# Second half of a fused kernel on one core: instruction order from a list of deadlines, four more buffers, and weight sums one stage behind

## The chip, the cores and the metric

One core of a Trainium2 chip runs the whole program; the other cores are idle. The metric is the device time of one execution in microseconds (us), and the kernel before stands at 1070.38 us (median of 3 runs, 1067.11 to 1073.82). All times below that are not called medians come from one profiled execution of the kernel before.

## What is computed

Three stages follow each other on 2304 tokens of width 512.

```
# attention: 4 batches, 8 heads, 576 positions, head size 64
out_up    = repeat(softmax(q4 @ k4.T / 8) @ v4, 4)   # q4, k4, v4: means of 4 neighbours
out_local = softmax(q @ k.T / 8 where |i-j| < 4) @ v
x = out_up + out_local                               # [2304, 512]
# gated FFN, 512 -> 1536 -> 512
xn = x / sqrt(mean(x*x) + 1e-6) * rms_g
x  = (silu(xn @ w_gate) * (xn @ w_val)) @ w_out
# squared-relu FFN, 512 -> 2048 -> 512
r  = maximum(x @ w_in, 0)
y  = (s * r * r + b) @ w_out2
```

Weights arrive in double precision. The kernel widens them on the chip and splits every number into two halves of 16 bits, a high and a low one, so a product costs three matmuls (high·high, high·low, low·high).

## The kernel before

**Tiling.** Tokens are worked in 8 blocks of 288 (TB), each as two halves of 144 (HB). The middle of x is kept transposed in Xf (4 row tiles of 128, trace name X).

**First part.** Attention for 4 batches runs as generators beside the first gated FFN. The FFN's blocks 0 and 1 run together, 2 to 5 one after the other (`middle`), 6 and 7 together (`mains`). A gate or value tile is 12 matmuls at L577, the elementwise work on it is at L584, L585 and L187 (ScalarE ACT, VectorE DVE), the output tiles are 36 matmuls each at L599, and a row sum `sn` per block (L619, reduced at L621) gives the block's scale `xsc`. From step START_W of the middle blocks on (`open_w2`), TensorE (PE), ACT and DVE run in the order in which the code issues them; before that a scheduler orders ACT and DVE.

**Side work.** Beside blocks 2 to 7, `side_work` prepares the second FFN's weights in 8 parts q (0 to 3 are w_in, 4 to 7 are w_out2). A part is: four raw pieces (a DMA at L476 into one of three staging buffers, two ACT instructions L480 and L481, two DVE instructions L485 and L487; piece n+3 is fetched only when piece n is through DVE), block sums t1, t3, t2 (DVE L887, L888, L895) for a product scheme with 7 instead of 8 block products, 16 small matmuls into `st` (L894) whose row maximum `mi` (L898) gives a power-of-two scale (L181 to L183), a last block sum (L899), and 14 conversions into halves, each one ACT instruction (L133) and one DVE instruction (L134) that depend on each other. All steps of a part are issued before the next part's raw pieces, except that the next part's first ACT pair is issued after conversion 10. `side_step` issues a side step at 2 of 3 FFN steps and later at each. `open_at` holds the parts 4 to 7 back until the first FFN has done with the storage they overwrite.

**Second part.** Per block, the in stage computes 4 groups p (512 columns of the hidden layer each) with 7 products of 12 matmuls each (`product`, L1012, 128x128 weights on 144 columns). The products accumulate in three PSUM banks per group (pa and pb from a pool of 4, pc from a pool of 2). ACT copies pa (L1042 or L1026), DVE adds to the banks' contents (L1017, reads pb and pc), ACT applies relu and square (L1026, L1027; in odd groups one square is on DVE), and the combinations (L1017, L1020, L1024) are turned into halves `G` ("put": ACT L133, DVE L134). The y stage has 7 products of 4x12 matmuls on G, in banks ya, yd, yb, yc; results leave through ACT (L1096) and a DMA (L1098). `x_parts` builds the next block's operand xo from Xf during the y stage. Only PE is in hand order here; the scheduler orders ACT and DVE. Groups 2 and 3 use three scratch buffers of groups 0 and 1 again (SETS: SL[1], SL[3], SL[4] and SL[6], SL[8], SL[9]), so their first writes wait for the last put of group 0 or 1. A bank of pb or pc is used by PE again only when DVE has read its earlier content. The side work's last steps are issued between the products of block 0.

Of the kernel before, what the change touches and what calls it, by code (L numbers as in the profile page):

```python
# [8 lines left out]
F32 = mybir.dt.float32  # L9
# [15 lines left out]
TB = 288  # L25
# [23 lines left out]
START3 = 16  # L49
START_W = 84  # L50
# [29 lines left out]
def kernel(  # L80
# [751 lines left out]
    def side_work():  # L832
# [26 lines left out]
        for n in range(3):  # L859
            issue(n)  # L860
        yield
        for q in range(8):
            c = chain(q)
            for kc in range(KC):
                n = q * KC + kc
                while not open_at(q, "raw", kc):
                    yield
                if n not in acted:
                    first(n)
                    yield  # L870
                if kc < 3:
                    first(n + 1)
                if wide:
                    widen_dve(stgs[n % 3], c.f32(kc * 512, 512))
                issue(n + 3)
                if q >= 4:
                    f = c.f32(kc * 512, 512)
                    if n == 16:
                        pool.tensor_copy(out=tail["csum"], in_=f)
                    else:  # L880
                        pool.tensor_tensor(out=tail["csum"], in0=tail["csum"], in1=f, op=ALU.add)
                yield
            while not open_at(q, "T"):
                yield
            r = c.f32(0, PART).rearrange("p (u c) -> p u c", c=256)
            t1, t2, t3, b22 = r[:, 8:10], r[:, 10:12], r[:, 12:14], r[:, 5:8:2]
            dve.tensor_tensor(out=t1, in0=r[:, 1:4:2], in1=r[:, 0:3:2], op=ALU.subtract)  # L887
            dve.tensor_tensor(out=t3, in0=r[:, 1:4:2], in1=b22, op=ALU.subtract)  # L888
            yield
# [5 lines left out]
            dve.tensor_tensor(out=t2, in0=b22, in1=t1, op=ALU.subtract)  # L895
            yield
            mi = p1.tile([128, 1], F32, tag="mi", name="mi")
            dve.tensor_reduce(out=mi, in_=st, axis=AX.X, op=ALU.max)  # L898
            dve.tensor_tensor(out=r[:, 1:4:2], in0=r[:, 4:7:2], in1=t2, op=ALU.subtract)  # L899
# [66 lines left out]
    if True:  # L966
# [17 lines left out]
        for _ in xparts:  # L984
            pass

    order[0].__exit__(None, None, None)
    tail["m2"].__exit__(None, None, None)
    order[0] = tc.manual_schedule(engines={pe.engine})
    order[0].__enter__()  # L990
# [4 lines left out]
    SL = [s12[:, i] for i in range(12)] + [R[:, 6112:6400], tail["csum"][:, :TB]]  # L995
# [6 lines left out]
    def product(ps, i, w, x, first, last_):  # L1002

        b = UNIT[PAIRS[i][1]]
        n = len(x)
        for j in range(n):
            for m in range(2):
                for k in range(2):
                    for lw, lx in ((0, 0), (0, 1), (1, 0)):
                        t, o = w[j]  # L1010
                        a = 2 * o + b[k] * 512 + lw * 256 + 128 * m
                        pe.matmul(out=ps[:, m, :], lhsT=t[:, a:a + 128], rhs=x[j][:, i, lx, k, :],  # L1012
                                  start=first and j == m == k == lw == lx == 0,
                                  stop=last_ and j == n - 1 and k == 1 and lw == 1, skip_group_check=True)
# [4 lines left out]
    def sub(o, a, b):
        dve.tensor_tensor(out=o, in0=a, in1=b, op=ALU.subtract)  # L1020

    def square(o, src, eng):
        if eng is dve:
            dve.scalar_tensor_tensor(out=o, in0=src, scalar=0.0, in1=src, op0=ALU.max, op1=ALU.mult)  # L1024
        else:
            act.activation(out=o, in_=src, func=AF.Relu)  # L1026
            act.activation(out=o, in_=o, func=AF.Square)  # L1027

    def in_stage(blk):

        def put(p, i, src):
            halves(G[p][:, i, 0], G[p][:, i, 1], src, gsc[:, p:p + 1], dve)

        def group(p):
            s = [two(t) for t in SETS[p]]
            w, x = [(W2h, p * PART)], [xo]
            a, b = (mmp.tile([128, 2, HB], F32, tag="mm", name="p" + n) for n in "ab")
            c = pC.tile([128, 2, HB], F32, tag="c", name="pc")
            product(a, 0, w, x, True, False)
            product(b, 1, w, x, True, False)  # L1040
            product(c, 2, w, x, True, False)
            act.activation(out=s[0], in_=a, func=AF.Copy)  # L1042
            add(s[2], b, s[0])
            yield
            product(b, 3, w, x, False, False)
            product(a, 4, w, x, False, True)
            add(s[3], b, s[0])
            add(s[3], c, s[3])
            square(s[1], a, act)
            put(p, 0, s[1])  # L1050
            yield
            product(c, 5, w, x, False, True)
            product(b, 6, w, x, False, True)
            square(s[3], s[3], act)
            put(p, 6, s[3])
            add(s[0], b, s[0])
            add(s[2], c, s[2])
            square(s[2], s[2], dve if p % 2 else act)
            put(p, 4, s[2])
            square(s[0], s[0], act)  # L1060
            yield
            sub(s[1], s[0], s[1])
            add(s[4], s[0], s[3])
            add(s[3], s[3], s[1])
            put(p, 1, s[3])
            put(p, 2, s[4])
            sub(s[2], s[2], s[3])
            put(p, 5, s[2])
            put(p, 3, s[1])

        rest_ = []
        for p in (0, 2):
            pair = [group(p), group(p + 1)]
            for k in range(3):
                for g in pair:
                    next(g)
                    yield
                if k == 0:
                    for g in rest_:
                        next(g, None)  # L1080
            rest_ = pair
        later.extend(rest_)

    later = []

    def y_stage(blk):
        t0 = blk * TB
        w = [(W1h, PART * p) for p in range(3)] + [(Rh, 0)]
        keep = p1.tile([128, 2, TB], F32, tag="x2", name="keep")
        s1, c21 = two(keep[:, 0]), two(keep[:, 1])  # L1090
        v, c22 = two(SETS[0][0]), two(SETS[0][2])

        def emit(c, r, src):
            ys = two(p1.tile([128, TB], F32, tag="u", name="ys", bufs=3))
            for m in range(2):
                act.activation(out=ys[:, m], in_=src[:, m], func=AF.Identity,  # L1096
# [109 lines left out]
```

## Time and profile before

| | |
|---|---|
| median of 3 runs | 1070.38 us (1067.11 to 1073.82) |
| profiled execution | 1075.27 us, span of its trace 1073.5 us |
| PE busy | 961.5 us, 90% of the span |
| PE weight loads (beside the matmuls) | 826.6 us, 77% |
| DVE busy | 714.1 us, 67% |
| ACT busy | 605.3 us, 56% |
| POOL busy | 270.8 us, 25% |
| DMA | 61.44 MB, 18% of the queues' span |

Busy times are sums over the span, and overlapped pieces of pipelined matmuls count once. What counts for a change is not an engine's share of the whole span but, in each stretch, who waits for whom. In the rows further on, a bracket like [4.39 <-DVE R L1017] says that the engine stood idle for 4.39 us before that instruction, and that a DVE instruction of line 1017 with output R ended the wait. PEclk is the clock granted to PE, 1.00 being 2.4 GHz. W, W1 and R are the large SBUF tensors that hold weights, halves and scratch buffers.

### The profile page before, as it was taken

Reading aid. Unit: us, or ns where it says so; the run is one execution under the profiler, and the core shown is the slowest. Engines: PE = TensorE matmul, PEld = TensorE weight load, DVE = VectorE, ACT = ScalarE, POOL = GpSimd, SP = SyncE. Lnnn points to the kernel's source line nnn. Section 1 sums busy time; section 2 is a strip of 40 time slices with the busy share of each in tenths; the row PEclk is TensorE's granted clock in tenths of the full one; section 3 lists DMA queues with packets and bytes.
Section 4 is the critical chain, followed back from the end, with each engine's and each line's share of the span. In section 5 each row is a group of like instructions: output and inputs, shape, how many; then the busy total and the mean of one; then the engine's idle time right before and its main releaser. Section 6 shows DMA issues by size and latency. Waiting matters only on the chain.

```text
span 1073.5 us, 27144 instructions
## 1 busy us (share of the span) xinstructions
PE 961.5 (90%) x11342; PEld 826.6 (77%) x11347; DVE 714.1 (67%) x1652; ACT 605.3 (56%) x1486; POOL 270.8 (25%) x356
## 2 busy tenths in 40 slices
PE   5965999989999999999899887798989898989987
PEld 3654776768877888877678765798989898988887
DVE  4997986754443441577767787967585958586674
ACT  2865685634434442456544556757574847566573
POOL 7524754544463333311114331000000000000000
PEclk8976999999999999999989998989989998999899
DMA  8873054211111000131212230000000000000000
GB/s 241 274 220 121 20 158 141 81 46 47 46 40 54 13 2 1 60 99 40 80 40 79 60 87 33 2 8 18 19 7 24 2 24 2 24 7 18 7 19 24
DMA packets 25579, 61.44 MB, mean 57 GB/s; under 512 B 3216, under 2 KB 11408, under 8 KB 25456
## 3 DMA queue, kind: packets, MB, share of 16 engines
q1 hardware_dynamic: 25456, 59.70, 18.3%
q8 instruction: 89, 1.46, 0.6%
q14 instruction: 34, 0.28, 0.1%
HBM read 54.97 MB, written 4.72 MB: 56 GB/s over the span
## 4 chain that ended last, share of the span: by engine, by line
PE 58%; DVE 22%; ACT 9%; DMA 6%; issue 3%; POOL 2%; SPq 0%; ACTq 0%; DVEq 0%; POOLq 0%
PE mmb L577 14%; DVE W L134 8%; PE mmb L599 7%; PE yc L1012 5%; PE ya L1012 4%; PE yb L1012 4%; PE pb L1012 4%; PE pc L1012 4%; DVE R L1017 3%; ACT W L133 3%; PE m2b L577 3%; PE yd L1012 2%; PE pa L1012 2%; DMA R<-in_moe_w_out_dram 2%; DMA R<-in_moe_w_val_dram 1%
## 5 line engine op out<-in xcount | busy, mean ns | idle before, releaser
L1012 PEld LDWEIGHTS <-W 128*128 128x128 f16 x4704 | 313.0, 101 | 42.8 <-issue 41.4
L577 PEld LDWEIGHTS <-W 128*128 128x128 f16 x2304 | 224.8, 99 | 63.8 <-issue 5.3
L577 PE MATMUL mmb<-X,W 128*128 128x288 f16 x1800 | 244.8, 291 | 3.0 <-ACT X L450 1.1
L599 PEld LDWEIGHTS <-W 128*128 128x128 f16 x1152 | 113.2, 100 | 34.5 <-ACT W L133 2.3
L589 POOL TENSOR_TENSOR R<-u,R 128x288 f16<-128x288 f32 x96 | 77.8, 811 | 201.0 <-ACT R L588 174.1
L599 PE MATMUL mmb<-R,W 128*128 128x288 f16 x864 | 115.2, 290 | 3.1 <-DVE u L585 2.0
L1012 PE MATMUL pc<-W,W 128*128 128x144 f16 x768 | 67.0, 244 | 35.2 <-DVE R L1017 34.3
L588 ACT ACTIVATE R<-u 128x288 f16<-128x288 f32 x96 | 42.2, 440 | 99.2 <-DVE u L187 99.1
L1012 PE MATMUL pb<-W,W 128*128 128x144 f16 x1152 | 95.5, 237 | 0.6 <-DVE R L1017 0.6
L134 DVE SCALAR_TENSOR_TENSOR W<-R,gsc,W 128x288 f16<-128x288 f32 x168 | 82.7, 518 | 2.7 <-ACT W L133 2.7
L133 ACT ACTIVATE W<-R,gsc 128x288 f16<-128x288 f32 x168 | 82.5, 525 | 3.0 <-DVE R L1020 2.6
L577 PE MATMUL m2b<-X,W 128*128 128x288 f16 x504 | 68.6, 286 | 0.0
L134 DVE SCALAR_TENSOR_TENSOR W<-W,wis 128x256 f16<-128x256 f32 x98 | 46.4, 505 | 29.1 <-ACT W L133 29.1
L585 DVE SCALAR_TENSOR_TENSOR u<-u,mmb 128x288 f32<-128x288 f32 x54 | 24.2, 450 | 56.1 <-PE mmb L577 54.2
L1017 DVE TENSOR_TENSOR R<-pb,R 128x288 f32<-128x288 f32 x88 | 40.3, 457 | 29.6 <-PE pb L1012 22.8
L1012 PE MATMUL pa<-W,W 128*128 128x144 f16 x768 | 59.1, 227 | 0.0
L133 ACT ACTIVATE W<-W,wis 128x256 f16<-128x256 f32 x98 | 45.3, 499 | 21.7 <-DVE wis L182 14.0
L584 ACT ACTIVATE u<-mmb,tsc 128x288 f32<-128x288 f32 x96 | 46.9, 490 | 15.6 <-PE mmb L577 14.7
L1096 ACT ACTIVATE ys<-R,bcol,cy 128x144 f32<-128x144 f32 x32 | 14.5, 500 | 70.2 <-DVE R L1017 57.6
L487 DVE SCALAR_TENSOR_TENSOR W<-W,R 128x512 int32<-128x512 int32 (+1 forms) x53 | 48.5, 916 | 1.3
L1027 ACT ACTIVATE R<-R 128x288 f32<-128x288 f32 x112 | 48.1, 436 | 1.2
L485 DVE SCALAR_TENSOR_TENSOR R<-R 128x512 int32<-128x512 int32 (+1 forms) x57 | 40.5, 710 | 9.3 <-ACT R L481 9.1
(245 smaller groups left out, 1721.3 us busy)
## 6 DMA issues: line engine op xcount, KB each, us to landing
R<-in_moe_w_out_dram SPq DMA_DIRECT2D x26, 512.0 KB
R<-in_moe_w_in_dram SPq DMA_DIRECT2D x16, 512.0 KB
qkT<-in_qk_dram SPq DMA_DIRECT2D x14, 576.0 KB
out_dram<-ys SPq DMA_DIRECT2D x32, 144.0 KB
vw<-in_vwin_dram SPq DMA_DIRECT2D x14, 315.0 KB
vd<-in_vgrp_dram SPq DMA_DIRECT2D x13, 288.0 KB
W<-in_moe_w_gate_dram SPq DMA_DIRECT2D x9, 384.0 KB
R<-in_moe_w_val_dram SPq DMA_DIRECT2D x8, 384.0 KB
```

The lines of the kernel that those rows point to most:

```text
L133: act.activation(out=hi, in_=src, func=AF.Copy, scale=scale)
L134: dve.scalar_tensor_tensor(out=lo, in0=src, scalar=scale, in1=hi, op0=ALU.mult, op1=ALU.subtract)
L485: dve.scalar_tensor_tensor(out=stg[:, :, 0], in0=stg[:, :, 1], scalar=-2 ** 31, in1=stg[:, :, 0], op0=ALU.bitwise_and, op1=ALU.bitwise_or)
L487: dve.scalar_tensor_tensor(out=di, in0=di, scalar=3, in1=stg[:, :, 0], op0=ALU.logical_shift_left, op1=ALU.bitwise_or)
L577: pe.matmul(out=acc, lhsT=Cgv.half(o, FP, lw)[:, f0 * 128:f0 * 128 + 128], rhs=X16[:, kc, 3 * blk:3 * blk + 3, lx, :], start=i == 0, stop= ...
L584: act.activation(out=u, in_=ps[0], func=AF.Tanh, scale=tsc[:, part:part + 1])
L588: act.activation(out=hi, in_=u, func=AF.Copy)
L589: pool.tensor_tensor(out=lo, in0=u, in1=hi, op=ALU.subtract)
L599: pe.matmul(out=acc, lhsT=Co.half(fc * 512, 512, lw)[:, m * 128:(m + 1) * 128], rhs=g16(fc)[:, lx, :], start=i == 0, stop=i == 35)
L1012: pe.matmul(out=ps[:, m, :], lhsT=t[:, a:a + 128], rhs=x[j][:, i, lx, k, :], start=first and j == m == k == lw == lx == 0, stop=last_ and ...
L1017: dve.tensor_tensor(out=o, in0=a, in1=b, op=ALU.add)
L1027: act.activation(out=o, in_=o, func=AF.Square)
```

## The change

**Second part.** Its instructions are no longer issued directly. `in_stage`, `x_ops` (for `x_parts`) and `y_stage` add them to a list with the buffers that they read and write and a duration. `Plan.order` gives each ACT and DVE instruction a deadline: PE's own order is laid out at 0.0626 us per matmul without a gap, and from there the deadlines run backward through the dependences. Then it fills the three engines in time: of the instructions whose inputs are ready the one with the earliest deadline goes first. All blocks are in one list; PE, ACT and DVE then run in that fixed order.

**Buffers.** Four more scratch buffers, SL[14] to SL[17], lie on block 0's columns of Xf (read before). Groups 2 and 3 get two of them each. All squares are on ACT. In the y stage products 2, 5, 3 become 2, 3, 5, and results are written into scratch buffers instead of tiles `ys`.

**Side work.** It is drained before the second part begins. `convert(q)` (maximum, last sum, scale, 14 conversions) runs while the raw pieces of part q+1 are widened; `gram(q)` (the matmuls into `st`) is issued one side step later than before, or at the second raw piece of the next part. `side_step` runs 3 of 4 steps, attention's last batch starts at step 12 instead of 16 (START3), and the hand order with the side work at step 76 instead of 84 (START_W).

The constants and `side_step`:

```diff
-START3 = 16
-START_W = 84
+START3 = 12
+START_W = 76
...
-        if free or tail["n"] % 3 != 2:
+        if free or tail["n"] % 4 != 3:
             next(tail["side"], None)
```

The end of a part q in `side_work` (`pending` holds the steps of `convert(q - 1)` that are left; one of them also runs where a raw piece has to wait):

```diff
+                if kc == 1:
+                    gram(q - 1)
...
+            dve.tensor_tensor(out=t1, in0=b12, in1=b11, op=ALU.subtract)
+            dve.tensor_tensor(out=t3, in0=b12, in1=b22, op=ALU.subtract)
+            yield
+            dve.tensor_tensor(out=t2, in0=b22, in1=t1, op=ALU.subtract)
+            first((q + 1) * KC)
+            yield
+            for n, _ in enumerate(pending):
+                if n == 0:
+                    gram(q)
+                yield
+            pending = convert(q)
+        gram(7)
+        yield
+        yield from pending
```

The buffers of the four groups:

```diff
-    SETS = [(SL[0], SL[1], SL[2], SL[3], SL[4]), (SL[5], SL[6], SL[7], SL[8], SL[9]),
-            (SL[10], SL[1], SL[11], SL[3], SL[4]), (SL[12], SL[6], SL[13], SL[8], SL[9])]
...
+    SL += [Xf[:, kc, :TB] for kc in range(KC)]
+    SETS = [(0, 1, 2, 3, 4), (5, 6, 7, 8, 9), (10, 14, 11, 15, 4), (12, 16, 13, 17, 9)]
```

`Plan.order`, deadlines and choice, one of the operations with its two durations (time on the engine, time until its output can be read; a put has 0.43 and 0.6 on either engine), and the squares of a group:

```diff
+            for k in pes:
+                late[k] = t
+                t += self.ops[k][3]
+            for k in reversed(range(n)):
+                if self.ops[k][0] != PEe:
+                    late[k] = min([late[j] for j in succ[k]] + [t + 9.0]) - self.ops[k][4]
...
+                    t0 = max(free[e], min(rdy.values()))
+                    k = min((k for k in c if rdy[k] <= t0), key=lambda k: (late[k], k))
+                    if best is None or t0 < best[0]:
+                        best = (t0, e, k)
...
+    def tt(o, a, b, op):
+        plan.add(DVEe, lambda: dve.tensor_tensor(out=slot(o), in0=get(a), in1=slot(b), op=op), [nm(a), b], [o], 0.38, 0.55)
...
-            square(s[2], s[2], dve if p % 2 else act)
...
+            for j in (2, 0):
+                actv(s[j], s[j], AF.Relu)
+                actv(s[j], s[j], AF.Square)
```

The loop over the blocks:

```diff
+    for _ in tail["side"]:
+        pass
...
+    for blk in range(NB):
+        in_stage(blk)
+        if blk == 0:
+            finish_out2()
+        if blk < NB - 1:
+            x_ops(blk + 1)
+        y_stage(blk)
+    plan.emit()
```

**The steady block on DVE.** The first place is DVE in block 1 of the second part, at the last products of groups 2 and 3. Before (pb_9594 and pc_9595 are the banks of group 2, pb_9635 is one of group 3; X_84 rows belong to x's operand, gsc rows are puts):

```order
L1017 TENSOR_TENSOR csum_5809<-pb_9635,R_83 128x288
L134 SCALAR_TENSOR_TENSOR W1_82<-X_84,xsc_73,W1_82 128x288
L1017 TENSOR_TENSOR R_83<-R_83 128x288
L134 SCALAR_TENSOR_TENSOR W1_82<-R_83,gsc_1089,W1_82 128x288 x5
L1020 TENSOR_TENSOR R_83<-R_83 128x288
L134 SCALAR_TENSOR_TENSOR W1_82<-R_83,gsc_1089,W1_82 128x288
L1017 TENSOR_TENSOR R_83<-pb_9594,R_83 128x288
L134 SCALAR_TENSOR_TENSOR W1_82<-X_84,xsc_73,W1_82 128x288
L134 SCALAR_TENSOR_TENSOR W1_82<-R_83,gsc_1089,W1_82 128x288
L1017 TENSOR_TENSOR R_83<-pb_9635,R_83 128x288
L134 SCALAR_TENSOR_TENSOR W1_82<-R_83,gsc_1089,W1_82 128x288
L1017 TENSOR_TENSOR R_83<-pc_9595,R_83 128x288
```

Now (bmm_9592 and bc_9608 are the banks b and c of group 2, bmm_9639 and bc_9654 those of group 3):

```order
L1145 TENSOR_TENSOR R_83<-bmm_9592,R_83 128x288
L1156 SCALAR_TENSOR_TENSOR W1_82<-R_83,gsc_1089,W1_82 128x288
L1145 TENSOR_TENSOR mask_68<-bmm_9639,R_83 128x288
L1156 SCALAR_TENSOR_TENSOR W1_82<-R_83,gsc_1089,W1_82 128x288
L1145 TENSOR_TENSOR R_83<-R_83 128x288 x2
L1145 TENSOR_TENSOR X_84<-bmm_9592,R_83 128x288
L1145 TENSOR_TENSOR R_83<-R_83 128x288
L1145 TENSOR_TENSOR X_84<-bc_9608,X_84 128x288
L1145 TENSOR_TENSOR R_83<-R_83 128x288
L1145 TENSOR_TENSOR X_84<-bmm_9639,R_83 128x288
L1145 TENSOR_TENSOR R_83<-R_83 128x288
```

Before, ten puts, two combinations and two reads of pb stood between group 3's first read of its bank b (csum<-pb_9635) and group 2's read of pc_9595; now a put, three combinations and one read stand between the same two reads (mask<-bmm_9639 and X<-bc_9608), and the reads of the c banks go into new buffers.

**The side work on DVE.** The second place is part q=6 on DVE, near the end of the first part. Before (W_82 is the part's storage, wis its scale):

```order
L887 TENSOR_TENSOR W_82<-W_82 128x512
L888 TENSOR_TENSOR W_82<-W_82 128x512
L895 TENSOR_TENSOR W_82<-W_82 128x512
L621 TENSOR_REDUCE mo<-sn 128x1
L181 TENSOR_SCALAR poh<-mo 128x1
L182 TENSOR_SCALAR pos<-poh 128x1
L183 TENSOR_SCALAR poi<-pos 128x1
L623 COPY xsc<-pos 128x1
L187 SCALAR_TENSOR_TENSOR cx<-bigo,poi 128x1
L898 TENSOR_REDUCE mi<-st 128x1
L899 TENSOR_TENSOR W_82<-W_82 128x2x256
```

Now, with the last raw piece of part 6 ahead of it:

```order
L485 SCALAR_TENSOR_TENSOR R<-R 128x512
L487 SCALAR_TENSOR_TENSOR W_82<-W_82,R 128x512
L935 TENSOR_TENSOR W_82<-W_82 128x512
L936 TENSOR_TENSOR W_82<-W_82 128x512
L938 TENSOR_TENSOR W_82<-W_82 128x512
L134 SCALAR_TENSOR_TENSOR W_82<-W_82,wis 128x256 x13
L880 TENSOR_REDUCE mi<-st 128x1
L881 TENSOR_TENSOR W_82<-W_82 128x2x256
```

The sums L935 to L938 are followed by 13 conversions of part 5, and only then by part 6's maximum L880; before, the maximum came right behind the sums and a block's scale.

**The handover on DVE.** The third place is where the second part begins. Before, reads of banks and conversions of part 7 alternate:

```order
L1017 TENSOR_TENSOR R<-pb,R 128x288
L912 TENSOR_SCALAR gsc<-mm__8561,big 128x4
L134 SCALAR_TENSOR_TENSOR R<-R,wis 128x256
L187 SCALAR_TENSOR_TENSOR cy<-cx,c_8471 128x8
L134 SCALAR_TENSOR_TENSOR R<-R,wis 128x256
L1017 TENSOR_TENSOR R<-pb,R 128x288
L134 SCALAR_TENSOR_TENSOR R<-R,wis 128x256
L1017 TENSOR_TENSOR R<-pc,R 128x288
```

Now all of part 7's conversions, a block's scale and three combinations of x (L1224) stand ahead of the first read of a bank (L1145):

```order
L134 SCALAR_TENSOR_TENSOR R<-R,wis 128x256 x3
L621 TENSOR_REDUCE mo<-sn 128x1
L181 TENSOR_SCALAR poh<-mo 128x1
L182 TENSOR_SCALAR pos<-poh 128x1
L183 TENSOR_SCALAR poi<-pos 128x1
L623 COPY xsc<-pos 128x1
L187 SCALAR_TENSOR_TENSOR cx<-bigo,poi 128x1
L134 SCALAR_TENSOR_TENSOR R<-R,wis 128x256 x7
L187 SCALAR_TENSOR_TENSOR c_8500<-s_sb,big 128x1
L187 SCALAR_TENSOR_TENSOR cy<-cx,c_8500 128x8
L1224 TENSOR_TENSOR tu<-X 128x288 x2
L1224 TENSOR_TENSOR tu<-X,tu 128x288
```

The next DVE row behind these is the first read of a bank, `L1145 TENSOR_TENSOR R<-bmm,R`.

## Rows read from the trace of the kernel before

**Rows 1.** Windows of the span; columns are named in the first line

```profile
core 0: us, PE busy (x) PEld busy (x) DVE busy (x) ACT busy (x) POOL busy (x), PEclk, DMA share, GB/s
0.00:442.68 442.68, 396.06 (x4242) 307.01 (x4248) 260.83 (x626) 227.50 (x587) 213.19 (x297) 0.94 0.30 91
442.68:620.65 177.97, 167.39 (x1390) 133.38 (x1388) 130.93 (x259) 96.30 (x214) 44.16 (x49) 0.98 0.23 72
620.65:725.90 105.25, 88.50 (x1011) 78.66 (x1008) 85.58 (x196) 66.15 (x157) 13.49 (x10) 0.92 0.10 29
725.90:774.73 48.83, 43.89 (x676) 43.63 (x674) 34.37 (x83) 30.94 (x76) 0.00 (x0) 0.97 0.05 14
725.90:1068.43 342.53, 309.57 (x4707) 307.54 (x4704) 235.94 (x570) 213.65 (x525) 0.00 (x0) 0.96 0.05 14
1068.43:1073.50 5.07, 0.00 (x1) 0.00 (x0) 0.82 (x2) 1.70 (x4) 0.00 (x0) 0.91 0.19 59
```

**Rows 2.** Waits of PE, 672 to 1074 us: total us, times, longest us

```profile
PE pc L1012 <- DVE R L1017: 34.3, 8, 5.2
PE yc L1012 <- DVE R L1017: 4.4, 8, 0.5
```

**Rows 3.** Timeline of PE, block 1: start us, duration us, instructions [idle before]

```profile
726.65 0.91 PE L1012 MATMUL pb<-W,W 128*128 128x144 f16 x12
...
743.15 0.91 PE L1012 MATMUL pa<-W,W 128*128 128x144 f16 x12
748.46 1.60 PE L1012 MATMUL pc<-W,W 128*128 128x144 f16 x12 [4.39 <-DVE R L1017]
...
753.02 2.41 PE L1012 MATMUL ya<-W 128*128 128x144 f16 x36
...
768.73 2.41 PE L1012 MATMUL yc<-W 128*128 128x144 f16 x36 [0.55 <-DVE R L1017]
```

**Rows 4.** Timeline of DVE while PE waits in block 1

```profile
742.99 2.23 DVE L134 SCALAR_TENSOR_TENSOR W<-R,gsc,W 128x288 f16<-128x288 f32 x5
...
745.93 0.46 DVE L1017 TENSOR_TENSOR R<-pb,R 128x288 f32<-128x288 f32 x1
...
747.94 0.46 DVE L1017 TENSOR_TENSOR R<-pc,R 128x288 f32<-128x288 f32 x1
```

**Rows 5.** Groups by line, blocks 1 to 7: busy us, mean ns, idle before

```profile
L134 DVE SCALAR_TENSOR_TENSOR W<-R,gsc,W 128x288 f16<-128x288 f32 x147 | 72.2, 518 | 2.7 <-ACT W L133 2.7
L133 ACT ACTIVATE W<-R,gsc 128x288 f16<-128x288 f32 x147 | 72.0, 524 | 3.0 <-DVE R L1020 2.6
...
L1027 ACT ACTIVATE R<-R 128x288 f32<-128x288 f32 x98 | 42.0, 436 | 1.1
...
L1017 DVE TENSOR_TENSOR R<-R 128x288 f32<-128x288 f32 x56 | 25.4, 454 | 0.0
```

**Rows 6.** Waits of PE, 442.68 to 672 us

```profile
PE st L894 <- DVE W L487: 13.3, 7, 3.7
PE st L894 <- DVE R L487: 6.4, 3, 2.9
```

**Rows 7.** Timeline of PE and DVE, 620 to 665 us: pieces of the side work

```profile
623.07 0.45 DVE L187 SCALAR_TENSOR_TENSOR u<-u,mmb 128x288 f32<-128x288 f32 x1
...
625.06 4.57 PE L599 MATMUL m2b<-R,W 128*128 128x288 f16 x36
...
644.12 0.68 DVE L895 TENSOR_TENSOR W<-W 128x512 f32<-128x512 f32 x1
...
649.16 0.88 DVE L134 SCALAR_TENSOR_TENSOR W<-W,wis 128x256 f16<-128x256 f32 x2 [0.26 <-ACT W L133]
650.28 0.88 DVE L134 SCALAR_TENSOR_TENSOR W<-W,wis 128x256 f16<-128x256 f32 x2 [0.24 <-ACT W L133]
...
662.64 0.69 DVE L487 SCALAR_TENSOR_TENSOR R<-R 128x512 int32<-128x512 int32 x1
```

**Rows 8.** The chain that ended last: start us, us, what

```profile
634.70 3.62 DMA R<-in_moe_w_out_dram
```

More of the change, by code (lines that the diff above doesn't have):

```diff
@@ L857, in first, with gram @@
                 sp.dma_start(out=dst, in_=source(n))
[L859 to L862, printed above, removed]
+        grams = {}
+        def gram(q):
+            if q < 0 or q in grams:
+                return
             c = chain(q)
[L864 to L889, printed above, removed]
             st = wide_mm[0].tile([128, 512], F32, tag="st", name="st")
@@ L1004, in product, with fn @@
+    def product(ps, i, w, x, xn, first, last_):
         b = UNIT[PAIRS[i][1]]
-        n = len(x)
-        for j in range(n):
+        t, o = w
+        def fn():
+            p = ps()
             for m in range(2):
@@ L1019, in sub @@
[L1019 to L1027, printed above, removed]
+                        pe.matmul(out=p[:, m, :], lhsT=t[:, a:a + 128], rhs=x[:, i, lx, k, :],
+                                  start=first and m == k == lw == lx == 0,
+                                  stop=last_ and k == 1 and lw == 1, skip_group_check=True)
@@ L1029, in in_stage @@
+    ADD, SUB = ALU.add, ALU.subtract
     def in_stage(blk):
[L1031 to L1032 removed]
         def group(p):
[L1035 to L1043, printed above, removed]
[L1044 to L1069 removed]
@@ L1086, in y_stage @@
     def y_stage(blk):
         t0 = blk * TB
[L1088 to L1094, printed above, removed]
-            for m in range(2):
-                act.activation(out=ys[:, m], in_=src[:, m], func=AF.Identity,
-                               bias=bcol[:, 2 * c + m:2 * c + m + 1], scale=cy[:, blk:blk + 1])
-            sp.dma_start(out=out[256 * c:256 * c + 256, t0 + HB * r:t0 + HB * r + HB].rearrange("(m p) t -> p m t", p=128),
-                         in_=ys)
@@ L1114, in y_stage, with product_ @@
[L1114 to L1129 removed]
+        wy = [(W1h, PART * p) for p in range(3)] + [(Rh, 0)]
+        def product_(ps, i, first, last_):
+            for p in range(NPART):
+                product(ps, i, wy[p], G[p], f"G{p}.", first and p == 0, last_ and p == NPART - 1)
@@ L1135, in finish_out2 @@
     def finish_out2():
-        bps = pY.tile([128, KC], F32, tag="y", name="bps")
-        for m in range(KC):
-            pe.matmul(out=bps[:, m:m + 1], lhsT=tail["csum"][:, 128 * m:128 * m + 128], rhs=ones_f[:, 0:1],
-                      start=True, stop=True)
-        act.activation(out=bcol, in_=bps, func=AF.Copy, scale=b_sb[:, 0:1])
-        mul(c1, s_sb, 2.0 ** 42, big[:, 0:1])
-        mul(cy, cx, c1[:, 0:1], cx)
-    for blk in range(NB):
-        for n, _ in enumerate(in_stage(blk)):
-            if blk == 0 and n >= 1:
-                next(tail["side"], None)
-                while "gsc" not in tail:
-                    next(tail["side"])
-                if n == 5:
-                    finish_out2()
-        if blk == 0:
-            for _ in tail["side"]:
-                pass
-        xp = x_parts(blk + 1) if blk < NB - 1 else iter(())
-        for n, _ in enumerate(y_stage(blk)):
-            if n == 0:
-                for g in later:
-                    next(g, None)
-                del later[:]
-            if n >= 2:
-                next(xp, None)
-                next(xp, None)
-        for _ in xp:
-            pass
+        bps = Bank("y")
@@ new lines, in fn @@
+        def fn():
+            t = bps().rearrange("p m t -> p (m t)")
+            for m in range(KC):
+                pe.matmul(out=t[:, m:m + 1], lhsT=tail["csum"][:, 128 * m:128 * m + 128], rhs=ones_f[:, 0:1],
+                          start=True, stop=True)
+        plan.add(PEe, fn, ["csum"], [bps.name], 0.45, 0.7)
+        plan.add(ACTe, lambda: act.activation(out=bcol, in_=bps().rearrange("p m t -> p (m t)")[:, :KC], func=AF.Copy,
+                                              scale=b_sb[:, 0:1]), [bps.name], ["bcol"], 0.3, 0.4)
```

274 lines of the change are left out of this document (219 added, 55 removed).

## The prediction

> **What bounds the kernel now.** I read the windows first, then PE's waits, then the timelines of PE and DVE at one wait, then the groups by line for prices. The windows [rows 1] show PE busy for nearly the whole of every stretch, so time can only be won where PE waits or runs at a lower clock. In blocks 1 to 7 of the second part, 342.53 us long, a block takes 48.9 us. PE's waits [rows 2] name one cause for most of what is lost there: 8 waits, 34.3 us, at a product into a pc bank, ended by DVE's read of that bank at L1017. The timeline of block 1 [rows 3] shows the place: 24 products run without a break, the 25th (at 748.46) stands 4.39 us. In that time DVE is not idle [rows 4]: it works off five puts in one row (742.99, 2.23 us) and reaches the read of pc only at 747.94. So the wait is one of order. DVE has the capacity: 34.37 us busy in a block of 48.83 [rows 1]. The first half has a second wait of this kind, smaller: the small matmuls into `st` stand 13.3 + 6.4 = 19.7 us for the last raw piece of a weight part [rows 6].
>
> **The floor of a block.** A product of 12 matmuls takes 0.75 us (block 1 starts at 725.90, its second product at 726.65 [rows 1, 3]), 0.0626 us a matmul. A block has 28 products in the in stage and 28 in the y stage: 56 x 0.75 = 42.0 us. Seven blocks: 294.0, against 342.53: at most 48.5 us to win. The Trainium skill, TensorE: Matmul & The Clock Gate, section Back-to-back issue gap, gives about 81 ns a matmul for a stream of weight load and matmul pairs with 128 columns. An estimate by it would be a floor of 54.4 us a block, and nothing to win here; the time would then be about 1053. Block 1 took 48.83 us with its waits, so the trace contradicts it, and the row decides.
>
> **Part A: blocks 1 to 7.** I walked the new order on DVE against PE's need. The 25th product needs group 2's c bank read by 24 x 0.75 = 18.0 us after the block's start. The read depends on an add that can start when the 21st product ends, at 15.75; behind it stand one more combination and the read. With 0.37 us for the first two, 0.46 for the read (L1017 takes 454 ns [rows 4, 5], and I count the next one as starting 0.08 earlier) and 0.2 for two handovers, it ends at about 17.2: 0.8 us to spare. Group 3's is wanted at 19.5 and ends at 18.7, the same. Before, that read had fourteen instructions behind group 3's first read of b, now five. The y stage has more room: results are needed only at the next use of a bank, 3 us later, and the old wait at yc (4.4 us in 8 [rows 2]) comes from the same backlog. The load fits: DVE has 81 instructions a block (83 before, two squares moved away), some 33.5 us; ACT gets 4 more (76 + 4 = 80), 30.94 + 4 x 0.436 = 32.7 us [rows 1, 5], 78% of 42.0. These four cost nothing while ACT's 9.3 us of free time in a block hides them; without that cover they are 1.7 us a block. Since 0.8 us is two DVE instructions, I keep 0.5 us a block, one late read of 0.46: gain 48.5 - 7 x 0.5 = **45.0**. Bounds: nothing left, 48.5; or a wait of 1.5 us each block plus the products behind it at a lower clock. In block 1 the four products behind the wait took 753.02 - 748.46 = 4.56 instead of 3.0, since PE came out of the wait at 1.60 us for the first instead of 0.91 [rows 3]. So 3 us a block, gain 27.5. The four buffers are part of this: without them the reads would wait for the last puts of groups 0 and 1.
>
> **Part B: from 620.65 to the end of block 0** (105.25 us before [rows 1]; times from 620.65 on). PE: 8 output tiles at 4.41 each (620.65 to 625.06 [rows 1, 7]) are 35.3; two parts' matmuls into `st` and two row sums, 32 x 0.0626 + 8 x 0.1225 = 3.0. So the second part could start at 38.3. In the new order gram(7) stands 60 output matmuls ahead of the end: PE is there at 38.3 - 60 x 0.1225 - 1.5 = 29.4. DVE: its last gate tile ends at 2.9 [rows 7]; scale 0.8, one conversion 0.6, a raw piece 1.9, three sums 2.0 (0.68 each [rows 7]), 13 conversions at 0.56 (a pair of conversions in 1.12, from 649.16 to 650.28 [rows 7]) 7.3, and 1.6 where ACT has PE's tiles to evict: 17.1. Maximum, last sum and scale 2.0, seven conversions 3.9, a block's scale 1.3, three conversions 1.7, first raw piece of part 7 1.4 (two instructions of 0.69 [rows 7]): 27.4. Only then is the fourth piece of part 7 fetched: 3.6 for its DMA [rows 8], 1.3 on ACT, 1.4 on DVE: 33.9 (with 0.2 of handovers). PE waits 4.5 there (29.4 to 33.9) and starts the second part at 42.8; before it was at 51.3. But now all of part 7's conversions stand ahead of DVE's first read of a bank: three sums 2.0, 18 conversions 10.1, x's first operand 4.5, maximum and sum 1.3, scales 1.9, block 7's scale 1.3, three combinations 1.1, the read 0.5, breaks for ACT 2.0: 24.7, so that the read ends at 58.6. PE needs it for its 7th product, at 42.8 + 6 x 0.75 = 47.3, and waits 11.3. Then 50 products, 37.5, and 2.8 for twice four products at the lower clock: block 0 ends at 98.9. Gain **6.4**. What the side work wins ahead of the second part, the handover mostly takes back. Bounds: 2 (4.4 us more on DVE or ACT, both in strict turn) to 11 (no breaks, conversions at 0.45, the pace of five puts in a row [rows 4]).
>
> **Part C: 442.68 to 620.65.** PE is idle 177.97 - 167.39 = 10.6 us, and the clock of 0.98 [rows 1] costs 3.6: 14.2 in all, most of it the waits at `st` [rows 6]. Now a part's raw pieces and the last part's conversions share the steps, and the matmuls into `st` stand at least one side step further behind the last piece; steps are 12 matmuls, 1.5 us, and the waits were at most 3.7 long [rows 6], after which one wait of about 2 us per two parts may stay. I keep 4.2 and count a gain of **10.0**; bounds 5 (half the waits only move) and 13.
>
> **The rest.** The scheduler also reorders loads and elementwise work in the opening, where PE is idle 442.68 - 396.06 = 46.6 us [rows 1]. Starting attention's last batch four steps earlier adds nothing to do; PE is busy there. I take 0, with 5 either way. The tail after the last product is 5.07 us [rows 1]; with the y products in another order, one add and one result less hang on the last: **0.8**.
>
> **Sum.** 45.0 + 6.4 + 10.0 + 0.8 = 62.2. The profiled run took 1075.3 us (1.8 us outside its span), 4.9 above the median of the runs; like it the new kernel would take 1013, and against the median 1070.4 - 62.2 = 1008.
>
> **Rivals.**
> *First, fixed order leaves a wait in each block.* DVE and ACT now run a list made from fixed durations; where a real one is longer, all that stands behind the late instruction is late too, and 0.8 us is little. For it: the puts are a chain of ACT and DVE, and [rows 5] show DVE waiting on L133. Against it: DVE and ACT are both a fifth idle. 3 us a block remain: 27.5 instead of 45.0, 1025.7. The Trainium skill, TensorE: Matmul & The Clock Gate, specification table, says of ScalarE and VectorE that their queues are strict first in, first out; [rows 4] agree, where a ready read of pc waits behind five puts.
> *Second, the handover is worse.* Part 7 is prepared with nothing of the second part between; if ACT's evictions and conversions take 12 us more in a row than in my walk, B is -6, and if the conversions delay the raw pieces, C is 5: 45 - 6 + 5 + 0.8 = 44.8, 1025.6.
> *Third, the list doesn't do what it says.* If the reads of pc are late through dependences and not through order, A is about 4 and the time 1049. [Rows 4] speak against it: the read starts without DVE having been idle before it.
> *Fourth, slower: ACT becomes the bound.* All squares and puts are on it, 80 instructions a block. Others gain 17.2, so the kernel is slower than before once a block takes over 48.9 + 17.2 / 7 = 51.4 us, that is 0.64 us an ACT instruction. [Rows 5] show 0.436 and 0.524, so it would need waits on DVE between most pairs; at 0.70 a block is 56.0, 7 x 7.1 = 49.5 lost, and the time 1070.4 + 49.5 - 16.4 = 1103.
>
> **Chances.** Forecast 0.60; first rival 0.18; second 0.10; third 0.05; fourth 0.04; anything else 0.03, counted as no change. The likeliest case's own range is 995 to 1019. The range goes down to all upper bounds together, 48.5 + 11 + 13 + 5 + 0.8 = 78.3, 992, and up past the first two rivals to 1030, which leaves the other three out. About 1% is what a measurement of this kernel can tell from no change: faster is below 1059.7. Faster 0.93, same 0.03, slower 0.04.
>
> **What would show it.** In the new profile: blocks 1 to 7 near 42.5 us each, with no wait at a c bank over 1 us (A); one wait of about 11 us at the second part's 7th product, ended by DVE, behind a second part that starts 8 us earlier (B); the waits at `st` between 442 and 620 us nearly gone (C). PE waiting for ACT, or for a bank in every block by 1.5 us or more, would show the first or fourth rival. A different stretch ahead of 440 us by more than 5 us would show that the opening was not nothing.

## The result, and the profile after

The changed kernel takes 1022.04 us (median of 4 runs, 1018.77 to 1023.97) against 1071.72 for the kernel before beside it: a ratio of 0.954 with a 95% interval of 0.950 to 0.958. A second set of runs gave 0.953 (0.951 to 0.956). 49.7 us were won; the forecast was 62.2 (1008 us), in a range of 992 to 1030.

The profiled execution has a span of 1022.2 us (1073.5 before). The page's first part shows what moved: PE and DVE are busy for less time, ACT for more.

```profile
span 1022.2 us, 27131 instructions
...
PE 946.5 (93%) x11347; PEld 812.3 (79%) x11347; DVE 705.4 (69%) x1636; ACT 611.3 (60%) x1518; POOL 272.3 (27%) x356
```

These are windows of the changed kernel, cut at the same events as [rows 1]: the same tile of the gated FFN (442.68 before, 442.10 now), block 6's first output tile (620.65, 620.46), the start of block 1 and of block 2 of the second part (725.90 and 774.73, now 723.73 and 765.73), and the last product's end (columns as in [rows 1]).

```profile
0.00:442.10 442.10, 396.43 (x4247) 306.92 (x4248) 266.06 (x636) 230.47 (x592) 215.13 (x297) 0.93 0.32 96
442.10:620.46 178.36, 169.29 (x1391) 134.26 (x1389) 123.79 (x250) 95.18 (x210) 42.33 (x49) 0.97 0.20 62
620.46:723.73 103.27, 86.60 (x1011) 77.19 (x1009) 87.34 (x198) 66.78 (x161) 14.83 (x11) 0.92 0.10 28
723.73:765.73 42.00, 42.00 (x676) 42.00 (x674) 33.29 (x81) 31.54 (x80) 0.00 (x0) 1.00 0.06 16
723.73:1017.73 294.00, 294.00 (x4707) 293.97 (x4704) 227.75 (x553) 217.97 (x553) 0.00 (x0) 1.00 0.06 16
1017.73:1022.20 4.47, 0.16 (x3) 0.00 (x0) 0.46 (x1) 0.90 (x2) 0.00 (x0) 0.80 0.33 98
```

Stretch by stretch against [rows 1]:

| stretch | before | after | won | forecast |
|---|---|---|---|---|
| opening | 442.68 | 442.10 | 0.6 | 0 |
| to block 6's output (C) | 177.97 | 178.36 | -0.4 | 10.0 |
| to the end of block 0 (B) | 105.25 | 103.27 | 2.0 | 6.4 |
| blocks 1 to 7 (A) | 342.53 | 294.00 | 48.5 | 45.0 |
| tail | 5.07 | 4.47 | 0.6 | 0.8 |
| span | 1073.5 | 1022.2 | 51.3 | 62.2 |

Blocks 1 to 7 have nothing left to win with this number of matmuls: PE is busy for 294.00 of 294.00 us at a granted clock of 1.00. Ahead of the second part almost nothing was won. PE's waits there (from 445.3 to 723.7 us) show why: the waits at `st` of [rows 6], 19.7 us, have become others.

```profile
PE sn L619 <- ACT x L605: 11.0, 3, 8.2
PE st L869 <- DVE mi L880: 7.0, 3, 3.6
PE st L869 <- DVE W L487: 4.4, 1, 4.4
PE mmb L599 <- ACT R L588: 1.2, 1, 1.2
PE st L869 <- DVE R L487: 0.9, 1, 0.9
```

Of the 19.7 us, 10.1 stood in the stretch of C before; there PE now waits 7.0 us for the maximum and 2.1 us at output tiles, for ACT and POOL. The row sums' 11.0 us and the other two rows at `st` lie in the stretch of B.

**Blocks 1 to 7, read closely.** The timelines of PE and of DVE in block 1 answer to [rows 3, 4]. The block starts at 723.73; the 25th product, the one that stood 4.39 us before, starts at 741.73, which is 18.0 us after the block's start, without a bracket.

```profile
738.73 3.16 PE L1127 MATMUL bmm<-W,W 128*128 128x144 f16 x48
741.73 0.91 PE L1127 MATMUL bc<-W,W 128*128 128x144 f16 x12
```

```profile
738.24 0.46 DVE L1145 TENSOR_TENSOR mask<-bmm,R 128x288 f32<-128x288 f32 x1 [1.01 <-PE bmm L1127]
738.61 0.51 DVE L1156 SCALAR_TENSOR_TENSOR W<-R,gsc,W 128x288 f16<-128x288 f32 x1
739.04 0.82 DVE L1145 TENSOR_TENSOR R<-R 128x288 f32<-128x288 f32 x2
739.77 0.45 DVE L1145 TENSOR_TENSOR X<-bmm,R 128x288 f32<-128x288 f32 x1
740.14 0.45 DVE L1145 TENSOR_TENSOR R<-R 128x288 f32<-128x288 f32 x1
740.51 0.45 DVE L1145 TENSOR_TENSOR X<-bc,X 128x288 f32<-128x288 f32 x1
...
741.97 0.45 DVE L1145 TENSOR_TENSOR X<-bc,X 128x288 f32<-128x288 f32 x1
```

The read of group 2's c bank ends at 740.51 + 0.45 - 723.73 = 17.2 us, as worked out, and 0.8 us ahead of its use; group 3's at 18.7 for a use at 19.5. DVE now waits for PE (1.01 us at 738.24), not PE for DVE.

### The profile page after: what moved, and what is told of

It is laid out like the page before. It is cut to its first block, busy times and chain, and to the rows that moved or that the text cites. A ratio compares the mean times of both kernels' runs of the same rounds, so it can differ in the third digit from the quotient of the medians.

```text
span 1022.2 us, 27131 instructions
## 1 busy us (share of the span) xinstructions
PE 946.5 (93%) x11347; PEld 812.3 (79%) x11347; DVE 705.4 (69%) x1636; ACT 611.3 (60%) x1518; POOL 272.3 (27%) x356
## 5 line engine op out<-in xcount | busy, mean ns | idle before, releaser
L1127 PEld LDWEIGHTS <-W 128*128 128x128 f16 x4704 | 298.0, 98 | 8.9 <-issue 8.8
L577 PEld LDWEIGHTS <-W 128*128 128x128 f16 x2304 | 224.4, 99 | 62.9 <-issue 4.7
L599 PEld LDWEIGHTS <-W 128*128 128x128 f16 x1152 | 114.8, 101 | 44.1 <-ACT W L133 6.1
L1127 PE MATMUL bmm<-W,W 128*128 128x144 f16 x1920 | 133.2, 227 | 0.3 <-DVE R L1145 0.3
L1127 PE MATMUL bc<-W 128*128 128x144 f16 x1152 | 77.2, 226 | 0.0
L577 PE MATMUL m2b<-X,W 128*128 128x288 f16 x552 | 75.1, 286 | 0.0
L1156 DVE SCALAR_TENSOR_TENSOR W<-R,gsc,W 128x288 f16<-128x288 f32 x136 | 68.0, 510 | 4.6 <-ACT W L1154 4.6
L1154 ACT ACTIVATE W<-R,gsc 128x288 f16<-128x288 f32 x136 | 68.8, 524 | 2.5 <-DVE R L1145 1.5
L1149 ACT ACTIVATE R<-R 128x288 f32<-128x288 f32 x160 | 62.6, 431 | 0.0
L1127 PE MATMUL bc<-W,W 128*128 128x144 f16 x768 | 59.0, 227 | 0.0
L1127 PE MATMUL by<-W 128*128 128x144 f16 x864 | 57.9, 226 | 0.0
L1145 DVE TENSOR_TENSOR R<-bmm,R 128x288 f32<-128x288 f32 x72 | 32.6, 453 | 33.8 <-PE bmm L1127 21.9
L133 ACT ACTIVATE W<-W,wis 128x256 f16<-128x256 f32 x98 | 45.1, 499 | 15.0 <-DVE W L134 10.6
L487 DVE SCALAR_TENSOR_TENSOR W<-W,R 128x512 int32<-128x512 int32 (+1 forms) x53 | 46.0, 868 | 1.4 <-ACT W L480 0.2
```

The lines of the kernel that those rows point to most:

```text
L133: act.activation(out=hi, in_=src, func=AF.Copy, scale=scale)
L487: dve.scalar_tensor_tensor(out=di, in0=di, scalar=3, in1=stg[:, :, 0], op0=ALU.logical_shift_left, op1=ALU.bitwise_or)
L577: pe.matmul(out=acc, lhsT=Cgv.half(o, FP, lw)[:, f0 * 128:f0 * 128 + 128], rhs=X16[:, kc, 3 * blk:3 * blk + 3, lx, :], start=i == 0, stop= ...
L599: pe.matmul(out=acc, lhsT=Co.half(fc * 512, 512, lw)[:, m * 128:(m + 1) * 128], rhs=g16(fc)[:, lx, :], start=i == 0, stop=i == 35)
L1127: pe.matmul(out=p[:, m, :], lhsT=t[:, a:a + 128], rhs=x[:, i, lx, k, :], start=first and m == k == lw == lx == 0, stop=last_ and k == 1 an ...
L1149: plan.add(ACTe, lambda: act.activation(out=slot(o), in_=get(a), func=func), [nm(a)], [o], 0.34 if psum else 0.42, 0.45 if psum else 0.52)
```

## The experiments

Ratios are to the kernel before, run on the same chip, with 95% intervals. "To the end of block 0" is counted from block 6's first output tile, in the profiled execution.

### Each half of the change by itself

*plan_alone*: the second part as changed, first part as before (`side_work` as a whole is the old one).

```diff
-START3 = 12
-START_W = 76
+START3 = 16
+START_W = 84
...
-        if free or tail["n"] % 4 != 3:
+        if free or tail["n"] % 3 != 2:
```

> The second part's list and buffers as changed, but the side work, START3, START_W and the 2-of-3 steps as before (still drained before the second part). Theory: blocks 1 to 7 take the floor, 294.0 us, by themselves, and the new side work brought nothing ahead of the second part (first row of block 6's output at 620.5 us in the changed kernel, 620.65 before), so the time is that of the changed kernel within what the old handover costs: 1020 to 1031 us. Rival: the new side work was worth its 10 us, hidden by a loss elsewhere; then this run is at 1032 or more.

Measured: 1022.59 us, 0.953 (0.950 to 0.957), the same as the whole change. Stretch by stretch too: 178.5 us for C, 103.8 for B and 294.0 for blocks 1 to 7, where the whole change has 178.36, 103.27 and 294.00. So 1.5 of the 2.0 us won in B come without the new side work.

*side_alone*: the opposite, the kernel before with the new side work and its three constants.

> The kernel before with the new side work, START3, START_W and the 3-of-4 steps; second part as before, with its waits of 34.3 + 4.4 us. Theory: no change, 1066 to 1076 us, because the waits at st for raw pieces are replaced by waits for the maximum of the part before (7.0 us in the changed kernel) and by row sums that wait for evictions on ACT (11.0 us). Rival, the prediction's term C: about 10 us faster, 1061.

Measured: 1073.39 us, 1.001 (0.999 to 1.003). No change. The waits of side_alone from 440 us on:

```profile
PE pc L1039 <- DVE R L1044: 32.1, 9, 4.4
PE sn L619 <- ACT x L605: 9.6, 3, 7.1
PE st L869 <- DVE mi L880: 7.0, 3, 3.6
PE yc L1039 <- DVE R L1044: 4.4, 8, 0.5
PE st L869 <- DVE W L487: 4.4, 1, 4.4
```

So all but some half a microsecond of the gain is the second part's, and term C was wrong. In plan_alone the old side work has its waits at `st` still (the last part's three: 8.1 us), and the handover shows up where the prediction put it for the changed kernel, at the 7th product, ended by DVE:

```profile
683.44 4.48 PE L1100 MATMUL bmm<-W,W 128*128 128x144 f16 x48 [7.92 <-DVE R L1118]
```

In the changed kernel about as much, 8.15 us, is lost a little earlier, at the row sum. With the old side work the second part starts 49.7 us after block 6's first output tile and block 0 takes 54.1 us; in the changed kernel it is 58.0 and 45.25.

### Order or buffers

*no_buffers*: the changed kernel without the four new buffers.

```diff
-    SETS = [(0, 1, 2, 3, 4), (5, 6, 7, 8, 9), (10, 14, 11, 15, 4), (12, 16, 13, 17, 9)]
+    SETS = [(0, 1, 2, 3, 4), (5, 6, 7, 8, 9), (10, 1, 11, 3, 4), (12, 6, 13, 8, 9)]
```

> The changed kernel with groups 2 and 3 using the scratch buffers of groups 0 and 1 again, as before (three each); the list is made anew for that. Theory that order alone decides: up to 1 us of wait a block, 1022 to 1030 us. Rival, that the buffers decide: the first writes of groups 2 and 3 come behind the last puts of groups 0 and 1, 2 to 4 us a block, 1037 to 1052 us.

Measured: 1029.38 us, 0.960 (0.956 to 0.963). Each block has one short wait; from one to the next it is 785.02 - 742.07 = 42.95 us instead of 42.00.

```profile
742.07 0.91 PE L1127 MATMUL bc<-W,W 128*128 128x144 f16 x12 [0.72 <-DVE R L1145]
785.02 0.91 PE L1127 MATMUL bc<-W,W 128*128 128x144 f16 x12 [0.72 <-DVE R L1145]
```

*before_buffers*: the kernel before with the four buffers alone, the scheduler ordering ACT and DVE.

```diff
+    SL += [Xf[:, kc, :TB] for kc in range(KC)]
...
-            (SL[10], SL[1], SL[11], SL[3], SL[4]), (SL[12], SL[6], SL[13], SL[8], SL[9])]
+            (SL[10], SL[14], SL[11], SL[15], SL[4]), (SL[12], SL[16], SL[13], SL[17], SL[9])]
```

> The kernel before with the four new buffers only: groups 2 and 3 use them, the scheduler still orders ACT and DVE. Theory that the old wait was one of order (removing the buffers from the changed kernel cost only 0.72 us of wait a block): the waits at pc stay, 28 to 36 us in sum, and the time is 1062 to 1074 us. Rival, that the old order was made by the buffers (the scheduler put the puts ahead because the reads' targets were not free): waits under 10 us, 1035 to 1045 us.

Measured: 1055.68 us, 0.986 (0.983 to 0.989), between the two expectations. The wait at pc is 3.11 instead of 4.39 us (its sum 23.9 instead of 34.3), a block 785.17 - 737.72 = 47.45 us:

```profile
737.72 1.60 PE L1013 MATMUL pc<-W,W 128*128 128x144 f16 x12 [3.11 <-DVE X L1018]
785.17 1.60 PE L1013 MATMUL pc<-W,W 128*128 128x144 f16 x12 [3.11 <-DVE X L1018]
```

So a block goes from 48.9 to 47.45 by the buffers alone, to 42.95 by the list without them, and to 42.00 by both: of 6.9 us the list is worth 6.0 by itself, the buffers 1.5 by themselves and 1.0 beside the list. "The list" includes here what came with it: the squares on ACT (tried below), and the y stage's products 2, 3, 5 and its results in scratch buffers, which no run takes apart; the old y stage's wait at yc delays its product by some 0.7 us a block in before_buffers as well. Neither theory's range was met. Most of the wait stays without the list, as the first has it, but the buffers also let the scheduler place the read earlier: between the first read of group 3's bank b and that of group 2's pc it now issues seven puts, where it issued ten.

*code_order*: all of the change, but the list is emitted in the order in which the code adds to it.

```diff
-            for k in self.order():
+            for k in range(len(self.ops)):
```

> The changed kernel with all four new buffers, but the list is emitted in the order in which the code adds it, without deadlines. Theory that order decides: seven puts of one group stand ahead of the reads of the next group's banks, and x's puts ahead of the y stage's reads; 4 to 10 us of wait a block, 1050 to 1090 us. Rival, that the buffers decide: at most 1 us a block, 1022 to 1030 us.

Measured: 1271.63 us, 1.186 (1.181 to 1.190), far more than the 4 to 10 us a block expected. The direction was as expected, the size was not: I had counted DVE's reads only, and ACT's order costs more in the y stage. Block 1's waits:

```profile
770.84 1.60 PE L1127 MATMUL bmm<-W,W 128*128 128x144 f16 x12 [4.67 <-DVE R L1145]
...
779.15 4.69 PE L1127 MATMUL bmm<-W,W 128*128 128x144 f16 x48 [5.27 <-DVE R L1145]
...
796.34 0.28 PE L1127 MATMUL by<-R 128*128 128x144 f16 x1 [7.25 <-ACT R L1154]
...
808.92 4.39 PE L1127 MATMUL by<-W 128*128 128x144 f16 x36 [6.98 <-ACT keep L1149]
```

Four waits, 24.2 us, fall in one block, 14.2 of them for ACT, and 7 more are lost in products behind them at a lower clock, 0.81 over the block (825.90 - 752.51 = 73.4 us for block 1, 31.4 over the floor). A fixed order alone is no gain; one made from deadlines is.

*squares_dve*: in each odd group one square on DVE again (one instruction) instead of on ACT (two).

```diff
+            if p % 2:
+                n2 = s[2]
+                plan.add(DVEe, lambda: dve.scalar_tensor_tensor(out=slot(n2), in0=slot(n2), scalar=0.0, in1=slot(n2),
+                                                                op0=ALU.max, op1=ALU.mult), [n2], [n2], 0.38, 0.55)
-            for j in (2, 0):
+            for j in ((0,) if p % 2 else (2, 0)):
```

> The changed kernel with one square in each odd group on DVE in one instruction, as before the change, instead of two on ACT; the list is made anew. Theory, that neither engine is the bound (33.3 and 31.5 us busy of 42.0 in a block): blocks 1 to 7 stay at 294.0 us and the time is that of the changed kernel, 1018 to 1025 us. Rival, that ACT's and DVE's balance made the difference: 0.5 us a block or more, 1025 to 1035 us.

Measured: 1020.78 us, 0.954 (0.952 to 0.955), the same as the changed kernel, with blocks 1 to 7 at 294.00 us. Beside this list, the squares' engine doesn't matter.

### The lost 10 us ahead of the second part

*early_max*: one DVE instruction moved, the maximum that reads part q-1's row of `st` (`largest` issues it once and keeps the result).

```diff
                 if kc == 1:
                     gram(q - 1)
+                if kc == 3:
+                    largest(q - 1)
...
-            dve.tensor_reduce(out=mi, in_=grams[q], axis=AX.X, op=ALU.max)
+            mi = largest(q)
```

> The changed kernel with one DVE instruction moved: the maximum of part q-1's row of st (which frees the one st bank) is issued right behind the fourth raw piece of part q, two sums and more ahead of where it was. Theory, that the 7.0 us of waits at st for mi come from that bank: they go, with the low clock behind them (block 4's first tiles ran at 2.06 instead of 1.47 us), 1011 to 1017 us. Rival, that DVE is late for everything there: the matmuls into st wait for raw pieces instead and the time is 1019 to 1024.

The place in the changed kernel, PE and then DVE: PE reaches the matmuls of a part at 505.83, the part's last raw piece is through DVE at 504.05 + 0.69, but PE starts only when L880 has read the bank.

```profile
508.91 1.89 PE L869 MATMUL st<-W 128*128 128x128 bf16 x16 [3.08 <-DVE mi L880]
510.60 2.23 PE L577 MATMUL mmb<-X,W 128*128 128x288 f16 x12
```

```profile
504.05 0.69 DVE L487 SCALAR_TENSOR_TENSOR W<-W,R 128x512 int32<-128x512 int32 x1
...
505.51 0.68 DVE L935 TENSOR_TENSOR W<-W 128x512 f32<-128x512 f32 x1
...
507.57 0.68 DVE L938 TENSOR_TENSOR W<-W 128x512 f32<-128x512 f32 x1
508.17 0.68 DVE L880 TENSOR_REDUCE mi<-st 128x1 f32<-128x512 f32 x1
```

There is one `st` bank. With the conversions a stage behind, the maximum of the part before, which frees it, stands behind this part's sums, so PE waits for an instruction that comes later than the one it waited for before. Measured for early_max: 1018.07 us, 0.952 (0.950 to 0.954), not told apart from the changed kernel; so it was run again beside it.

> The changed kernel once more, to stand beside the next ones on the same chip: 1018 to 1024 us. Blocks 1 to 7 at 294.0 us again.

> The kernel with the early maximum once more, since its profile showed 5.9 us less in the stretch up to block 6's output but its median only about 2 less than the changed kernel's. If the 5.9 us are real, it is 4 to 7 us under the changed kernel on this chip; if they were one execution's luck, under 2.

Measured: the changed kernel 1021.48 us, 0.953 (0.951 to 0.956); early_max 1015.68, 0.949 (0.947 to 0.950): 5.8 us less, intervals apart, where the first pair of medians showed about 2. The four profiles decide it, since the opening varies by more than that: from the tile at which the stretch of C starts to block 6's first output tile, the changed kernel takes 178.36 and 179.67 us, early_max 172.94 and 173.53, so 4.8 to 6.7 us less in every pairing. The waits for the maximum went from 7.0 to 2.2 us (6.7 and 1.8 in the other two profiles):

```profile
PE st L869 <- DVE mi L877: 2.2, 1, 2.2
```

That is the cause of about half of term C's miss.

### The handover

*conv_in_plan*: part 7's 14 conversions are in the list instead of ahead of it.

```diff
                 tail["gsc"] = True
+                tail["r"] = (c, r, sc)
+                return
...
+            plan.add(ACTe, lambda h=h, src=src: act.activation(out=h, in_=src, func=AF.Copy, scale=sc[:, 0:1]),
+                     [f"Rs{u}"], [f"Rh{u}"] + old, 0.42, 0.56)
...
+    r_ops()
     for blk in range(NB):
```

> The changed kernel with part 7's 14 conversions taken out of the drained side work and put into the list, with a dependence from the last y products of each part on them. Theory, that the handover is bound by DVE's and ACT's turn (the last row sum stood 8.15 us for an eviction behind conversions): the row sum's wait goes, the second part starts 6 to 9 us earlier, and block 0, with ACT at 40 of 42 us, gives up to 3 back: 1012 to 1018 us. Rival: the conversions crowd block 0 (28 more instructions on ACT and DVE) and the wait moves to its y stage: 1020 to 1026.

Measured: 1016.54 us, 0.950 (0.948 to 0.953), 3 to 4 us under the changed kernel's ratios; the intervals overlap, and the profile is clearer. The longest wait of the row sum falls from 8.15 to 3.25 us, and the end of block 0 comes 97.7 us after block 6's first output tile instead of 103.3 in both profiles of the changed kernel.

```profile
671.34 0.40 PE L619 MATMUL sn<-x,ones_b 128*128 128x288 bf16 x1 [3.25 <-ACT x L605]
```

*early_conv*: both edits.

> Both of the last two. If the two waits are separate places, the gains add: 1002 to 1011 us. If the second part's start is bound by the last raw pieces and not by either, at most one of them counts: 1012 to 1018.

Measured: 1011.34 us, 0.946 (0.943 to 0.948). That is 0.0077 under the changed kernel's 0.9534, 8.2 us: as far as ratios from different chips can tell, the gains of 2 to 6 and 3 to 4 add. In the profile both stretches are shorter, C with 173.4 us and B with 98.6.

*late_gram*: early_conv, and part 6's matmuls into `st` three side steps later.

```diff
-                if n == 0:
+                if n == (3 if q == 6 else 0):
                     gram(q)
```

> Early maximum and conversions in the list as in the run with both, and part 6's matmuls into st issued three side steps later. Theory: their wait of 4.4 us for the last raw piece goes, with the two tiles at a lower clock behind it (some 2 us): 1004 to 1009 us if the run with both stands at 1011. Rival: part 6's maximum comes later with them, the conversions of part 6 and the raw pieces of part 7 move back by as much, and nothing is won: 1010 to 1013.

Measured: 1010.52 us, 0.944 (0.943 to 0.946), the same as early_conv. The wait of 4.4 us at `st` is gone, and an earlier row sum has it instead:

```profile
640.20 0.40 PE L619 MATMUL sn<-x,ones_b 128*128 128x288 bf16 x1 [5.53 <-ACT x L605]
```

Nothing was won, as the rival of that run says; the row sum waits for ACT's eviction, so ACT and DVE are behind there, and PE's order is not what is wrong. early_conv and late_gram beat both kernels.

## Why the prediction was right, and where it was not

The time lies in the range, but above the 995 to 1019 us of the likeliest case. The range went to 1030 for two rivals, and neither came as described: no wait was left in the blocks, and B didn't turn into a loss, though C fell below the 5 us that the second gives it. A came out 3.5 us better than forecast, C 10.4 and B 4.4 worse.

**Part A** was right in its place and mechanism, and short by 3.5 us. The walk gave 17.2 and 18.7 us for the two reads, and the trace has 17.2 and 18.7. The step that was mis-sized is the 0.5 us a block kept for a late read: the 0.8 us of slack were never used up, and the residue is 0. The third rival (dependences, not order) falls with no_buffers and code_order; the first (a wait left in each block) and the fourth (ACT as the bound) fall with the windows, where ACT has 80 instructions and 31.5 us in a block, 32.7 forecast. The sentence that the reads would wait without the buffers was right in that a wait comes back, but it is 0.72 us, 1.0 with what follows it. (In the fourth rival, 7 x 7.1 is 49.7 and the others gain 17.2, not 16.4; its 1103 us stay.)

**Part C** was wrong: -0.4 where 10.0 stood, outside its own bounds of 5 to 13. The failed step is the sentence that the matmuls into `st` stand at least one side step further behind the last piece and so wait at most once in two parts. It looked only at their input. Of the 19.7 us of [rows 6] on which it drew, only 10.1 stood in this stretch to be won. The matmuls also write a bank, there is one, and its reader had moved behind two sums. Idle time fell by 1.5 us in this stretch (10.6 to 9.1 [rows 1]), and the clock went from 0.98 to 0.97, which by an estimate costs 178 x 0.01 = 1.8. early_max gave back 4.8 to 6.7 us of this stretch; what the rest hangs on was not tried.

**Part B** came out at 2.0 for 6.4, on its lower bound, and not by the way that was forecast. The second part was to start 8.5 us earlier (42.8 for 51.3) and block 0 to take 2.2 us longer; it started 6.7 us later (58.0), and block 0 took 45.25 us, 8.7 less than before. That the difference is still a gain is luck as far as this working goes. The walk on DVE failed at its first number: "its last gate tile ends at 2.9" was taken from the kernel before. In the new order two raw pieces of part 6 stand ahead of it, 4.6 us of DVE's time, and behind them part 5's maximum and last sum, 1.3 us:

```profile
621.16 1.19 DVE L485 SCALAR_TENSOR_TENSOR R<-R 128x512 int32<-128x512 int32 x1
622.38 1.11 DVE L487 SCALAR_TENSOR_TENSOR W<-W,R 128x512 int32<-128x512 int32 x1
623.42 0.68 DVE L485 SCALAR_TENSOR_TENSOR R<-R 128x512 int32<-128x512 int32 x1
624.13 1.64 DVE L487 SCALAR_TENSOR_TENSOR W<-W,R 128x512 int32<-128x512 int32 x1
...
628.22 0.45 DVE L187 SCALAR_TENSOR_TENSOR u<-u,mmb 128x288 f32<-128x288 f32 x1
```

It ends at 628.67, 8.2 us after block 6's first output tile: 5.3 late. The first read of a bank, forecast to start at 58.1, starts at 684.87, which is 64.4: 6.3 late, so most of that is the first step. Two more were off and cancel in part: the matmuls of part 6 into `st` waited 4.4 us, not counted, and those of part 7 waited 0.9 instead of 4.5. The wait of 11.3 us at the 7th product did not come; 8.15 us stand at the last row sum. The eviction that it needs stands on ACT behind conversions that DVE is late for: its tile is ready at 668.45, and ACT comes to it at 677.55. conv_in_plan, which takes the conversions away from there, cuts this wait to 3.25. The second part therefore starts at 678.48, 58.0 and not 42.8, and block 0 itself takes 45.25.

```profile
677.13 0.51 ACT L133 ACTIVATE R<-R,wis 128x256 f16<-128x256 f32 x1 [0.25 <-DVE R L134]
677.55 0.39 ACT L604 ACTIVATE X<-m2b 128x288 f32<-128x288 f32 x1
677.84 0.40 ACT L605 ACTIVATE x<-m2b 128x288 bf16<-128x288 f32 x1
```

```profile
678.29 0.40 PE L619 MATMUL sn<-x,ones_b 128*128 128x288 bf16 x1 [8.15 <-ACT x L605]
678.48 3.08 PE L1127 MATMUL bmm<-W,W 128*128 128x144 f16 x24
```

**The opening and the tail** came out as forecast (0.6 and 0.6, for 0 and 0.8). The opening itself varies: the tile that the changed kernel reached at 442.10 us came at 439.36 in its second profile (after_again), a difference of half the size of the early_max edit.

## What to carry to other kernels

Where PE waits for an engine that is busy but not full, first look at what stands ahead of the awaited instruction: a fixed list by deadlines, with the four buffers, closed the whole gap of 48.5 us here (some 42 of them without the buffers), while the same list in the code's order was 200 us slower than the kernel before. When work is moved a stage back, follow its outputs' buffers as well as its inputs: the instruction that frees a single bank moves too. A walk along an engine's new order has to start from that order's own rows, not from a time read in the old trace.

## What was not expected of the hardware

PE held one matmul of 128x128 on 144 columns, each with its own weight load, every 62.5 ns for 294 us without a gap, 4704 of them, at a granted clock of 1.00; before, with waits of 4.4 us once in a block, the same stretch had 0.96 [rows 1]. The Trainium skill, TensorE: Matmul & The Clock Gate, section Back-to-back issue gap, gives about 81 ns for such pairs at 128 columns; this trace doesn't agree. A wait of 0.72 us cost 0.95 in all. Behind the longer waits the next four products took 4.46 us (742.18 - 737.72, a wait of 3.11) and 4.56 (a wait of 4.39) instead of 3.00, so some 1.5 us more in either case. And DVE's L487 took 0.69 us at 619.69, when POOL was idle, but 1.64 at 624.13, while POOL's sum of the piece before was running (L927, 623.64 to 625.22); no run tests whether that is the cause.
